# Turning q, k, similarities and one-hots on VectorE in 32 by 32 blocks instead of on TensorE

## The chip, the cores and the metric

The kernel runs on one core of one Trainium2 chip. The metric is the device time of one launch in microseconds (us). A core has five engines that run their own instruction streams side by side and wait for each other through semaphores: TensorE (PE in the profile, its weight loads PEld), VectorE (DVE), ScalarE (ACT), GpSimd (POOL) and SyncE (SP), which here only issues transfers. SBUF is the on-chip memory of 128 partitions; PSUM is the memory that TensorE writes its results to.

## The reference

Two blocks follow each other. The first is routed attention: each query and each key is assigned to the nearest of 16 centroids of its head, and a query sees only the keys of its own centroid. The second sends each of the 3072 tokens through one of 8 experts.

```python
# B, H, S, D = 4, 8, 768, 64; 16 centroids a head
q_n, k_n, c_n = (each / (its norm + 1e-6))
q_assign = np.argmax(np.einsum('bhsd,hcd->bhsc', q_n, c_n), axis=-1)
k_assign = np.argmax(np.einsum('bhsd,hcd->bhsc', k_n, c_n), axis=-1)
mask = q_assign[:, :, :, None] == k_assign[:, :, None, :]
scores = scale * np.matmul(q, k.transpose(0, 1, 3, 2))      # scale = 1/sqrt(64)
scores = np.where(mask, scores, -1000000000.0)
attn = softmax(scores)                                       # with 1e-9 in the denominator
attn_out = np.matmul(attn, v)

x = attn_out.transpose(0, 2, 1, 3).reshape(3072, 512)
expert_idx = np.argmax(x @ w_gate, axis=1)                   # 8 experts
gate_w = the softmax probability of that expert
y = np.maximum(x @ w1[expert_idx], 0.0) @ w2[expert_idx]     # 512 -> 1024 -> 512
out = gate_w[:, None] * y
```

(Shortened: norms and the softmaxes are written out in the original, and the experts work on sorted rows.)

## The kernel before

The attention stage handles two heads at a time: there are 16 pairs `g`, and each pair has 12 units (two halves of 384 queries, six blocks of 128 keys). Six units make a turn, so a pair takes two turns, an even one and an odd one. In a turn TensorE first makes six blocks of scores, then part 0 of the turn's extra jobs, then the six sums over v, then part 1 of the jobs. The two heads lie side by side in the partitions, 64 each.

The mask is made by matmul: the one-hot of a query's centroid times (one-hot of the key's centroid - 1) x 2^60 is added to the score in the same PSUM bank, so that a key of another centroid gets about -2^60 and its exponential is 0.

```python
def score(u):
    ...
    ps = ps_s.tile([P, 2, 512], F32, name="sps")                 # three buffers
    for a in range(2):                                           # L855
        nc.tensor.matmul(ps[:, a, 0:HS], lhsT=qk[g][r, 1, ks], rhs=qk[g][r, 0, qs], start=True, stop=False)
    for a in range(2):                                           # L858
        nc.tensor.matmul(ps[:, a, 0:HS], lhsT=ohT[g][r, 1, ks], rhs=ohT[g][r, 0, qs], start=False, stop=True)
    A[u] = ap.tile([P, 2, HS], F32, name="A")                    # seven buffers
    nc.scalar.activation(A[u], ps[:, :, 0:HS], AF.Exp)           # L860
    if j == 1: ... T = A[u - 1] + 1e-9 / P + A[u]                # VectorE, L863
    elif j > 1: ... T = T + A[u]                                 # VectorE, L867
```

`qk` (head dimension in the partitions, tokens along) and `ohT` (centroids in the partitions, tokens along) have to be there a turn ahead. They are made by these jobs, one after the other:

```python
def turn(g, piece):        # transposes of q and k on TensorE, eight and then four
    ...
    for i in range(n):                                           # L770
        nc.tensor.transpose(ps[:, i * P : (i + 1) * P], rows[g, "qk"[w]][:, j]..., ident)
    if piece == 0:         # L777 (VectorE; for g == 1 L775, ScalarE) q times 1/8, L778 and L780 (ScalarE) k
        ...

def similar(g):            # similarities to the centroids
    for t in range(4):                                           # L787
        nc.tensor.matmul(ps[t * 2 * C : (t + 1) * 2 * C, 0:HS], lhsT=cblk[...], rhs=qk[g][...], ...)
    nc.vector.tensor_copy(sims[g], ps[:, 0:HS])                  # L792

def similar2(g):           # three transposes (L798), and a copy on ScalarE (L800)
    ...

def assign(g):             # L806 maximum, L807 who has it, L808 (GpSimd) a rank for the first of equals
    ...
def assign2(g):            # L814 the highest rank, L818 the one-hots (twice)
    ...

def put(g):                # six transposes of one-hots on TensorE (L828)
    ...
    nc.scalar.copy(oh[:, 0, :], ps[:, 0:S])                      # L833
    for a in range(2):                                           # L835
        nc.vector.tensor_scalar(oh[a * D : a * D + C, 1, :], ..., scalar1=BIG, scalar2=-BIG, ...)
```

The sums over v, the denominators with the gate's logits, and the rows of x:

```python
def attend(u):   # L875: O += v.T @ A, two heads
def finish(g, half):   # L883, ScalarE: O to SBUF
def weigh(g):    # L896: sums of T and x @ w_gate; L902 (ScalarE): to SBUF
def weigh2(g):   # three transposes (L909), copy L912, reciprocal L918, products L921, sums L928/L931 (VectorE)
def x_turn(g, half):   # three transposes (L941), scaled by 1/denominator L944 (VectorE)
def gate(b):     # L953 to L962: the gate, once in four pairs
```

And the order of the jobs, `at(turn, part, job)`, with `n = 2 * g`:

```python
    if g == 0:   # before the first turn
        at(-4, 0, turn, g, 0); at(-4, 1, turn, g, 1); at(-3, 0, similar, g); at(-3, 1, similar2, g)
    elif g == 1:
        at(-2, 1, turn, g, 0); at(-2, 1, turn, g, 1); at(-1, 1, similar, g); at(0, 0, similar2, g)
    else:
        at(n - 3, 0, turn, g, 0); at(n - 3, 0, turn, g, 1); at(n - 3, 1, similar, g); at(n - 2, 0, similar2, g)
    at(n - 2, 0, assign, g); at(n - 2, 0, assign2, g); at(n - 1, 0, put, g)
    at(n, 1, finish, g, 0); at(n + 1, 1, finish, g, 1)
    if g < NG - 1:
        at(n + 2, 0, weigh, g); at(n + 2, 1, weigh2, g); at(n + 2, 1, x_turn, g, 0); at(n + 3, 1, x_turn, g, 1)
        ... # after each fourth pair: gate (n + 3, part 0) and the rows of x to HBM
    ...
    at(max(n - 6, -1), 1, load_qk, g); at(max(n - 5, -1), 1, load_v, g)     # from g = 2 on
```

(Several calls are put on one line here.) Towards the end of the attention stage the routing of the first three batches is worked out in the same gaps (choose, count, slots, one-hots, tokens: L582 to L656), and then the experts follow (L310 and L364 first and second layer; L476 and L498 the same as seven products in place of eight; L291 to L299 the turning of gathered rows).

Of the kernel before, what the change touches and what calls it, by code (L numbers as in the profile page):

```python
# [185 lines left out]
def kernel(  # L186
# [80 lines left out]


# [10 lines left out]
    def turn_rows(g):  # L279

        full = len([m for m in g["n"] if m == P])
        for m, j0, j1 in ((P, 0, full), (RQ, full, len(g["n"]))):
            if j0 < j1:
                nc.scalar.copy(g["gate"][0:m, j0:j1], g["xg"][0:m, j0:j1, Dm])  # L284

        for j0 in range(0, len(g["n"]), 2):
            ms = g["n"][j0 : j0 + 2]
            tp = wide().rearrange("p a (c t) -> p a c t", t=P)
            for i, m in enumerate(ms):
                for c in range(DB):  # L290
                    nc.tensor.transpose(  # L291
                        tp[:, i, c, 0:m], g["xg"][0:m, j0 + i, c * P : (c + 1) * P], ident[0:m, 0:m]
                    )
            for i, m in enumerate(ms):
                dst = g["xT"][:, :, (j0 + i) * P : (j0 + i) * P + m]
                if i == 0:
                    nc.vector.tensor_copy(dst, tp[:, i, :, 0:m])  # L297
                else:
                    nc.scalar.copy(dst, tp[:, i, :, 0:m])  # L299

    def layer1(g, fbs):
# [3 lines left out]
        for f0 in range(fbs[0], fbs[1], 2 * per):  # L305
            hp = wide()
            for fb in range(f0, f0 + 2 * per):
                o = hp[:, (fb - f0) // per, (fb - f0) % per * cols : ((fb - f0) % per + 1) * cols]
                for c in range(DB):
                    nc.tensor.matmul(  # L310
                        o, lhsT=g["w"][0][:, c, fb * P : (fb + 1) * P], rhs=g["xT"][:, c, :cols],
                        start=(c == 0), stop=(c == DB - 1),
                    )
            for a in range(2):
                dst = g["h"][:, f0 + a * per : f0 + (a + 1) * per, :cols]
                src = hp[:, a, : per * cols].rearrange("p (f t) -> p f t", f=per)
                if a == 0 and not g.get("scalar_only"):
                    nc.vector.tensor_relu(dst, src)
                else:
                    nc.scalar.activation(dst, src, AF.Relu)  # L320
# [209 lines left out]
    def place_consts():  # L530
# [23 lines left out]
        nc.gpsimd.iota(tok_i, pattern=[[S, B], [1, NQ]], base=1, channel_multiplier=NQ)  # L554
        hl_i = consts.tile([P, 2, NT], I32, name="hl_i")
# [109 lines left out]
    with ExitStack() as actx:  # L665
# [17 lines left out]
        def load_qk(g):  # L683
            b, hp = divmod(g, HP)
            for name, src in (("q", q), ("k", k)):
                t = rows[g, name] = ld.tile([P, NQ, 2, D], F32, name=name + "_in")
                for a in range(2):
                    nc.sync.dma_start(out=t[:, :, a, :], in_=src[b, 2 * hp + a].rearrange("(p j) d -> p j d", j=NQ))
# [10 lines left out]
        nc.scalar.dma_start(out=csb, in_=centroids.rearrange("h c d -> (h c) d"))  # L699
        wg_in = consts.tile([P, DB, E], F32)  # L700
        nc.scalar.dma_start(out=wg_in, in_=moe_w_gate.rearrange("(a p) e -> p a e", p=P))
        for f in (load_qk, load_v):
            for g in range(2):
                f(g)
        make_identity(nc, ident)
        nc.vector.tensor_copy(ident_b, ident)

        ps = ps_m.tile([P, 512], F32, name="mps")
        for i in range(12):
            nc.tensor.matmul(ps[:, 0:P], lhsT=ident, rhs=ident, start=True, stop=True)  # L710
# [7 lines left out]
        nc.gpsimd.memset(one_row[:, E : E + 1], 1.0)  # L718
        for a in range(2):
# [3 lines left out]
        ohs = ohp.tile([P, NQ, 2, 2, 32], BF16, name="oh")  # L723
        nc.gpsimd.memset(ohs, 0.0)
        ohTs = []
        for i in range(2):
            t = ohp.tile([P, 2, S], BF16, name=f"ohT{i}")
            nc.gpsimd.memset(t[:, 1, :], 0.0)
            ohTs.append(t)

# [3 lines left out]
        nc.scalar.activation(csq, csb, AF.Square, accum_out=cs2)  # L734
# [15 lines left out]
        cps = ps_m.tile([P, 512], F32, name="mps")  # L750
        nc.tensor.transpose(cps[:, 0:P], cn.rearrange("p a d -> p (a d)"), ident)

        cblk = consts.tile([P, HP, 2, C], F32)
        nc.gpsimd.memset(cblk, 0.0)
        cview = cps[:, 0:P].rearrange("p (g a c) -> p g a c", a=2, c=C)
        for a in range(2):
            nc.vector.tensor_copy(cblk[a * D : (a + 1) * D, :, a, :], cview[a * D : (a + 1) * D, :, a, :])
# [4 lines left out]
        def turn(g, piece):  # L762
# [3 lines left out]
            ps = ps_s.tile([P, 2, 512], F32, name="sps").rearrange("p a c -> p (a c)")  # L766
            n = 4 if piece else 8
            for i in range(n):
                w, j = divmod(8 * piece + i, NQ)
                nc.tensor.transpose(ps[:, i * P : (i + 1) * P], rows[g, "qk"[w]][:, j].rearrange("p a d -> p (a d)"), ident)  # L770
            flat = qk[g].rearrange("p w s -> p (w s)")
            if piece == 0:

                if g == 1:
                    nc.scalar.mul(flat[:, 0:S], ps[:, 0:S], D**-0.5)  # L775
                else:
                    nc.vector.tensor_scalar_mul(flat[:, 0:S], ps[:, 0:S], D**-0.5)  # L777
                nc.scalar.copy(flat[:, S:1024], ps[:, S:1024])  # L778
            else:
                nc.scalar.copy(flat[:, 1024 : 2 * S], ps[:, 0 : 2 * S - 1024])  # L780

        def similar(g):
# [8 lines left out]
            sims[g] = asg.tile([P, HS], F32, name="simT", bufs=1)  # L791
            nc.vector.tensor_copy(sims[g], ps[:, 0:HS])  # L792

        def similar2(g):
            simT = sims.pop(g)
            ps = wide()[:, 0, :]
            for i in range(NQ // 2):
                nc.tensor.transpose(ps[:, i * P : (i + 1) * P], simT[:, i * P : (i + 1) * P], ident)  # L798
            sims[g] = asg.tile([P, G, C], F32, name="sim")
            nc.scalar.copy(sims[g], ps[:, 0:HS].rearrange("p (t c) -> p t c", c=C))  # L800

        def assign(g):

            sim = sims.pop(g)
# [3 lines left out]
            nc.gpsimd.tensor_tensor(sim, sim, first_c[:, None, :].to_broadcast([P, G, C]), op=ALU.mult)  # L808
            sims[g] = sim

        def assign2(g):
            rank = sims.pop(g)
            top = asg.tile([P, G], F32, name="top")
            nc.vector.tensor_reduce(top, rank, axis=AX, op=ALU.max)  # L814

            v = lambda t, w: t.rearrange("p (i w x) c -> p i w x c", w=2, x=4)[:, :, w]
            for w in range(2):
                nc.vector.tensor_tensor(  # L818
                    ohs.rearrange("p (i h) a w c -> p i (h a) w c", h=2)[:, :, :, w, 0:C], v(rank, w),
                    top.rearrange("p (i w x) -> p i w x", w=2, x=4)[:, :, w].unsqueeze(3).to_broadcast([P, NQ // 2, 4, C]),  # L820
                    op=ALU.is_equal,
                )

        def put(g):
            oh = ohT[g] = ohTs[g % 2]
            ps = wide()[:, 0, :].bitcast(BF16)
            for j in range(NQ):
                nc.tensor.transpose(  # L828
                    ps[:, j * P : (j + 1) * P],
                    ohs[:, (j % (NQ // 2)) * 2 + j // (NQ // 2)].rearrange("p a w c -> p (a w c)"), ident_b,  # L830
                )

            nc.scalar.copy(oh[:, 0, :], ps[:, 0:S])  # L833
            for a in range(2):
                nc.vector.tensor_scalar(  # L835
                    oh[a * D : a * D + C, 1, :], ps[a * D + 32 : a * D + 32 + C, 0:S],
                    scalar1=BIG, scalar2=-BIG, op0=ALU.mult, op1=ALU.add,
                )
# [9 lines left out]
        def score(u):  # L848
# [11 lines left out]
            nc.scalar.activation(A[u], ps[:, :, 0:HS], AF.Exp)  # L860
# [43 lines left out]
        def weigh2(g):  # L904
# [7 lines left out]
            nc.vector.tensor_copy(  # L912
# [6 lines left out]
            nc.gpsimd.tensor_copy(dens[:, g, :].rearrange("p (t a) -> p t a", a=2), den)  # L919
            lgh = stat.tile([P, NQ, 2, E], F32, name="lgh")  # L920
            nc.vector.tensor_tensor(  # L921
# [5 lines left out]
            if hp == 0:  # L927
                nc.vector.tensor_tensor(lgb, lgv[:, :, :, 0, :], lgv[:, :, :, 1, :], op=ALU.add)  # L928
            else:
                for a in range(2):  # L930
                    nc.vector.tensor_tensor(lgb, lgb, lgv[:, :, :, a, :], op=ALU.add)  # L931
# [49 lines left out]
        at(0, 1, place_consts)  # L981
        for g in range(NG):
            n = g * TG
            if g == 0:
                at(-4, 0, turn, g, 0)
                at(-4, 1, turn, g, 1)
                at(-3, 0, similar, g)
                at(-3, 1, similar2, g)
            elif g == 1:

                at(-2, 1, turn, g, 0)
                at(-2, 1, turn, g, 1)
                at(-1, 1, similar, g)
                at(0, 0, similar2, g)
            else:
                at(n - 3, 0, turn, g, 0)
                at(n - 3, 0, turn, g, 1)
                at(n - 3, 1, similar, g)
                at(n - 2, 0, similar2, g)
            at(n - 2, 0, assign, g)  # L1000
            at(n - 2, 0, assign2, g)
            at(n - 1, 0, put, g)
# [317 lines left out]
```

## Time and profile before

The median of three runs is 777.45 us (776.92 to 777.67).

| engine | busy us | share of the 776.7 us span |
|---|---|---|
| TensorE, matmul | 755.2 | 97% |
| VectorE | 449.8 | 58% |
| ScalarE | 299.0 | 38% |
| GpSimd | 111.0 | 14% |

| group | count | busy us |
|---|---|---|
| L855 scores (TensorE) | 768 | 160.6 |
| L875 sums over v (TensorE) | 768 | 130.9 |
| L860 exponentials (ScalarE) | 192 | 153.3 |
| L867 sums of weights (VectorE) | 128 | 122.7 |
| L770 transposes of q and of k (TensorE) | 192 | 13.2 and 13.1 |
| L787 similarities (TensorE) | 128 | 17.8 |
| L798 transposes of similarities (TensorE) | 48 | 8.7 |
| L828 transposes of one-hots (TensorE) | 96 | 8.4 |

A row of a timeline gives the start, the time until the end of the group, the engine, the line of the kernel, the operation, and what is written and read; xN is the number of instructions. A row of the waits says who waited for whom, the total in us, how often, and the longest.

### The profile page before, as it was taken

What the parts mean: (1) busy time and instruction counts of PE and PEld (TensorE: products, weight loads), DVE (VectorE), ACT (ScalarE), POOL (GpSimd) and SP (SyncE); (2) the same over time, 40 slices, a digit from 0 to 9 for tenths busy, and PEclk for the clock granted to TensorE, in tenths of its full rate; (3) what the DMA queues carried; (4) which work ended last, traced back from release to release, by engine and by line L of the source; (5) the groups of instructions that cost most, each with busy time, mean ns of one, the idle gap of its engine ahead of it and who ended that gap; (6) DMA issues with size and microseconds to landing.
All of it is one profiled execution on the core that took longest, in us unless ns stands there. A gap on an engine that the chain in (4) does not pass through costs nothing.

```text
span 776.7 us, 12417 instructions
## 1 busy us (share of the span) xinstructions
PE 755.2 (97%) x5021; PEld 485.7 (63%) x5021; DVE 449.8 (58%) x758; ACT 299.0 (38%) x481; POOL 111.0 (14%) x157
## 2 busy tenths in 40 slices
PE   6999999999999999999999999999999999999994
PEld 4544555445554455544556668787888898787861
DVE  3667677666676666778743544555564655555200
ACT  4545645556455564555531112232222214132210
POOL 2200000100000000001200541311312121211101
PEclk9999999999999999999999999999999999999998
DMA  9025501455115221120103446747556675847540
GB/s 221 6 62 204 136 26 37 144 208 131 30 33 144 62 62 31 32 103 1 45 1 135 152 127 224 267 166 253 221 216 219 246 261 178 308 155 246 212 156 18
DMA packets 85281, 106.41 MB, mean 137 GB/s; under 512 B 52831, under 2 KB 56927, under 8 KB 84704
## 3 DMA queue, kind: packets, MB, share of 16 engines
q1 hardware_dynamic: 79616, 85.99, 34.9%
q0 software_dynamic: 4928, 19.51, 6.8%
q8 instruction: 41, 0.67, 0.4%
q14 instruction: 24, 0.20, 0.1%
q10 hardware_dynamic: 672, 0.05, 0.1%
HBM read 92.90 MB, written 13.16 MB: 137 GB/s over the span
## 4 chain that ended last, share of the span: by engine, by line
PE 80%; issue 9%; DVE 6%; POOL 2%; ACT 2%; ACTq 0%; POOLq 0%; DVEq 0%
PE sps L855 15%; PE O L875 13%; PE sps L476 10%; PE sps L310 9%; PE sps L498 8%; PE sps L364 7%; PE sps L858 4%; PE mps L896 3%; DVE T L867 3%; PE sps L787 2%; PE sps L344 2%; PE sps L770 2%; PE sps L291 2%; PE sps L941 1%; PE mps L909 1%
## 5 line engine op out<-in xcount | busy, mean ns | idle before, releaser
L860 ACT ACTIVATE A<-sps 128x768 f32<-128x768 f32 x192 | 153.3, 812 | 53.4 <-PE sps L858 52.3
L855 PE MATMUL sps<-qk 64*128 64x384 f32 x768 | 160.6, 497 | 0.1
L867 DVE TENSOR_TENSOR T<-T,A 128x768 f32<-128x768 f32 x128 | 122.7, 959 | 14.4 <-ACT lsT L902 0.5
L875 PE MATMUL O<-A,v_in 128*64 128x384 f32 x768 | 130.9, 490 | 0.0
L855 PEld LDWEIGHTS sps<-qk 64*128 64x128 f32 x768 | 66.9, 189 | 50.4 <-issue 42.3
L875 PEld LDWEIGHTS O<-A,v_in 128*64 128x64 f32 x768 | 52.2, 137 | 62.6 <-issue 62.5
L858 PE MATMUL sps<-ohT 64*128 64x384 bf16 x384 | 63.6, 325 | 0.0
L364 PE MATMUL sps<-w,h_sb 128*128 128x512 f32 x144 | 63.1, 592 | 0.0
L310 PEld LDWEIGHTS sps<-xgT,w 128*128 128x128 f32 x512 | 58.3, 192 | 4.5 <-issue 2.5
L863 DVE SCALAR_TENSOR_TENSOR T<-A 128x768 f32<-128x768 f32 x32 | 30.7, 958 | 49.1 <-ACT A L860 49.1
L310 PE MATMUL sps<-xgT,w 128*128 128x128 f32 x512 | 58.7, 275 | 0.0
L328 POOL DMA_INDIRECT out_dram<-zo,s_idx x32 | 33.3, 1041 | 154.2 <-ACT zo L324 90.9
L274 POOL DMA_INDIRECT xg<-x_rows,g_idx x32 | 37.7, 1179 | 112.8 <-ACT gate L284 100.9
L808 POOL TENSOR_TENSOR sim<-sim,first_c 128x384 f32<-128x384 f32 x16 | 16.0, 999 | 264.2 <-DVE sim L807 264.2
L364 PEld LDWEIGHTS sps<-w,h_sb 128*128 128x128 f32 x144 | 26.7, 190 | 30.6 <-issue 30.6
L883 ACT COPY xT<-O 128x384 f32<-128x384 f32 x32 | 15.5, 483 | 62.1 <-PE O L875 62.0
L476 PEld LDWEIGHTS sps<-xs,w1s 128*128 128x128 f32 x288 | 36.0, 190 | 4.2 <-DVE xs L387 4.2
L476 PE MATMUL sps<-xs,w1s 128*128 128x144 f32 x288 | 37.8, 288 | 0.0
L324 ACT ACTIVATE zo<-sps,gate 128x512 f32<-128x512 f32 x12 | 8.2, 687 | 72.1 <-PE sps L364 60.1
L858 PEld LDWEIGHTS <-ohT 64*128 64x128 bf16 x384 | 19.5, 95 | 25.3 <-issue 0.6
L297 DVE COPY xgT<-sps 128x512 f32<-128x512 f32 (+1 forms) x20 | 10.8, 566 | 40.6 <-PE sps L291 40.6
L498 PE MATMUL sps<-w2s,hs 128*128 128x256 f32 x144 | 33.6, 383 | 0.0
(246 smaller groups left out, 988.2 us busy)
## 6 DMA issues: line engine op xcount, KB each, us to landing
w<-in_moe_w_dram SPq DMA_DIRECT2D x32, 2048.0 KB, 9.2
x_rows<-x POOLq DMA_DIRECT2D x4, 1548.0 KB, 6.5
q_in<-in_q_dram SPq DMA_DIRECT2D x32, 192.0 KB, 4.4
k_in<-in_k_dram SPq DMA_DIRECT2D x32, 192.0 KB, 4.8
v_in<-in_v_dram SPq DMA_DIRECT2D x16, 384.0 KB, 3.3
xg<-x_rows,g_idx POOLq DMA_INDIRECT x32, 4.5
out_dram<-zo,s_idx POOLq DMA_INDIRECT x32, 5.5
csb<-in_centroids_dram ACTq DMA_DIRECT2D x1, 32.0 KB, 1.9
```

Of the source, the lines that this page charges most:

```text
L274: nc.gpsimd.indirect_dma_start(out=g["xg"][0:m, j, :], out_offset=None, in_=x_d[0 : g["rows"], :], in_offset=bass.IndirectOffsetOnAxis(ap= ...
L310: nc.tensor.matmul(o, lhsT=g["w"][0][:, c, fb * P : (fb + 1) * P], rhs=g["xT"][:, c, :cols], start=(c == 0), stop=(c == DB - 1),)
L328: ins = nc.gpsimd.indirect_dma_start(out=out[:, :], out_offset=bass.IndirectOffsetOnAxis(ap=g["si"](j)[0:m], axis=0), in_=zo[0:m], in_offs ...
L364: nc.tensor.matmul(zp, lhsT=g["h"][:, fb, j * P : (j + 1) * P], rhs=g["w"][1][:, fb, :], start=(fb == 0), stop=(fb == FB - 1),)
L476: nc.tensor.matmul(o, lhsT=a[:, c, f * P : (f + 1) * P], rhs=b[:, c, :], start=(c == 0), stop=(c == KH - 1),)
L498: nc.tensor.matmul(ps[:, 0, 0:DH], lhsT=a[:, f, :], rhs=b[:, f, :], start=(f == 0), stop=(f == FH - 1),)
L855: nc.tensor.matmul(ps[:, a, 0:HS], lhsT=qk[g][r, 1, ks], rhs=qk[g][r, 0, qs], start=True, stop=False)
L858: nc.tensor.matmul(ps[:, a, 0:HS], lhsT=ohT[g][r, 1, ks], rhs=ohT[g][r, 0, qs], start=False, stop=True)
L860: nc.scalar.activation(A[u], ps[:, :, 0:HS], AF.Exp)
L863: nc.vector.scalar_tensor_tensor(T[g, half], in0=A[u - 1], scalar=1e-9 / P, in1=A[u], op0=ALU.add, op1=ALU.add)
L867: nc.vector.tensor_tensor(T[g, half], T[g, half], A[u], op=ALU.add)
L875: nc.tensor.matmul(O[g, half][a * D : (a + 1) * D, 0:HS], lhsT=rows[g, "v"][:, a, j, :], rhs=a_[:, a, :], start=(j == 0), stop=(j == NQ - 1),)
```

## The change

The transposes of q, k, the similarities and the one-hots leave TensorE. VectorE has a transpose of separate 32 by 32 blocks. To make whole transposes of blocks, the rows are loaded in another order: each 32 partitions hold 32 of the 64 head dimensions of one head, in pieces of 128 bytes. The one-hots come out of VectorE in blocks that lie in other partitions than the scores want, so eight small transfers a pair carry them to `ohT`. TensorE keeps the similarity matmuls. Each step is placed behind a turn's sums of weights and a turn or more ahead of its use.

```diff
 def load_qk(g):
+    for quad in range(4 if g else 0):
+        a, d0 = quad // 2, quad % 2 * 32
+        nc.sync.dma_start(
+            out=t[quad * 32 : (quad + 1) * 32]...,
+            in_=src[b, 2 * hp + a].rearrange("(m p i) d -> p i m d", m=4, i=NQ)[:, :, :, d0 : d0 + 32],
+        )
+    for a in range(0 if g else 2):       # pair 0 as before; its k on the ScalarE queue
...
+def turn_blocks(g):
+    for w in range(2):
+        nc.vector.transpose(qk[g][:, w, :], rows[g, "qk"[w]].rearrange("p j a d -> p (j a d)"))
...
 def similar(g):
-    nc.vector.tensor_copy(sims[g], ps[:, 0:HS])
+    nc.vector.transpose(sims[g], ps[:, 0:HS])
-def similar2(g): ...
...
 def assign2(g):
-    (one-hots by two is_equal into a padded tile)
+    nc.vector.tensor_tensor(groups_of(oh), rank, top..., op=ALU.is_equal)
+    nc.vector.transpose(sims[g], oh)
+def put_q(g):
+    for half in range(2):
+        for a in range(2):
+            nc.sync.dma_start(out=ohT[g][r, 0, cols], in_=sims[g][i])
+def put_k(g):
+    for a in range(2):
+        nc.vector.tensor_scalar(kv[D:P, a, :], t[D:P], scalar1=big[...], scalar2=big[...], ...)
+    for half in range(2):
+        for a in range(2):
+            nc.sync.dma_start(out=ohT[g][r, 1, (half * HS) : (half + 1) * HS], in_=kv[i, a, :])
...
-nc.scalar.activation(A[u], ps[:, :, 0:HS], AF.Exp)
+nc.scalar.activation(A[u], ps[:, :, 0:HS], AF.Exp, scale=D**-0.5)
...
 def weigh2(g):       # the copy L912 to ScalarE, products and sums L921 to L931 to GpSimd (not in the last pair)
...
 at(...):
     if g == 0:
-        turn, similar, similar2 from turn -4 on; assign and assign2 at -2, put at -1
+        at(-4, 0, turn, g, 0); at(-4, 0, load_next); at(-4, 0, blocks); at(-4, 1, turn, g, 1)
+        at(-3, 0, similar, g); at(-3, 0, assign, g); at(-3, 0, assign2, g); at(-3, 0, put, g)
     elif g == 1:
+        at(-2, 1, idle_of, 20)           # 20 matmuls whose result is not used
+        at(0, 0, turn_blocks, g)
+        for f in (similar, assign, assign2, put_q, put_k): at(0, 1, f, g)
     else:
-        at(n - 3, 0, turn, g, 0); at(n - 3, 0, turn, g, 1); at(n - 3, 1, similar, g); at(n - 2, 0, similar2, g)
+        at(n - 3, 0, turn_blocks, g)
+        at(n - 2, 0, similar, g); at(n - 2, 0, assign, g)
+        at(n - 2, 1, assign2, g); at(n - 2, 1, put_q, g); at(n - 2, 1, put_k, g)
```

(Cut: several lines are joined, and shapes are left out. Not shown: for the first pair the transposes of q and k stay on TensorE, and its one-hots, turned in blocks too, are copied to their place by ScalarE and VectorE; the rank of the first of equals is on VectorE for pairs 0 and 1; the squares of the centroids move from ScalarE to VectorE; the loads of pair 1 and of v wait until pair 0's k has landed; some constants are placed later.) A second part concerns two evictions of one PSUM tile: where VectorE takes the first half and ScalarE the second (the turning of gathered rows, and the expert's first layer), the second is now declared independent of the first.

## The prediction

> **What bounds the kernel now.** I read the busy shares first, then who waits for whom on TensorE, then the timeline of one pair of turns, then the costs of single groups.
>
> From the page of the kernel before (part 1: engine, busy us and share; part 2: TensorE by slices):
>
> ```profile
> PE 755.2 (97%) x5021; PEld 485.7 (63%) x5021; DVE 449.8 (58%) x758; ACT 299.0 (38%) x481; POOL 111.0 (14%) x157
> PE   6999999999999999999999999999999999999994
> ```
>
> TensorE (PE) is busy in every slice but the first and the last; the others have slack. Its waits over the whole run, longest total first:
>
> ```profile
> PE sps L828 <- DVE oh L818: 2.8, 1, 2.8
> PE sps L787 <- ACT qk L778: 2.4, 4, 0.8
> PE sps L787 <- DVE qk L777: 1.6, 2, 0.9
> ```
>
> That is 6.8 us in all on these three rows, so nearly everything that the change can win is TensorE work that goes away. What that work is stands in the timeline of TensorE in the attention stage (start, us, group):
>
> ```profile
> 67.14 0.92 PE L855 MATMUL sps<-qk 64*128 64x384 f32 x4
> ...
> 72.19 0.85 PE L896 MATMUL mps<-T,one_row 128*32 128x384 f32 x8
> ...
> 73.61 0.55 PE L798 MATMUL sps<-ident,simT 128*128 128x128 f32 x3
> 74.09 4.09 PE L875 MATMUL O<-A,v_in 128*64 128x384 f32 x24
> ...
> 78.92 0.92 PE L855 MATMUL sps<-qk 64*128 64x384 f32 x4
> ...
> 83.97 0.51 PE L828 MATMUL sps<-ident_b,oh 128*128 128x128 bf16 x6
> 84.31 0.83 PE L770 MATMUL sps<-ident,q_in 128*128 128x128 f32 x6
> 84.98 0.82 PE L770 MATMUL sps<-ident,k_in 128*128 128x128 f32 x6
> 85.72 4.09 PE L875 MATMUL O<-A,v_in 128*64 128x384 f32 x24
> 89.75 0.55 PE L941 MATMUL sps<-ident,xT 128*128 128x128 f32 x3
> 90.22 0.85 PE L787 MATMUL sps<-qk,cblk 128*32 128x384 f32 x8
> 91.01 0.92 PE L855 MATMUL sps<-qk 64*128 64x384 f32 x4
> ```
>
> One head pair is two turns: an even one of 78.92 - 67.14 = 11.78 us and an odd one of 91.01 - 78.92 = 12.09 us, 23.87 us together, with no gap between groups. Starts, not durations, give the cost, since ends overlap.
>
> Some odd turns are longer. The rows at one of them (bracket: idle before, and releaser):
>
> ```profile
> 332.20 1.33 PE L787 MATMUL sps<-qk,cblk 128*32 128x384 f32 x8 [0.53 <-ACT qk L778]
> 333.46 0.92 PE L855 MATMUL sps<-qk 64*128 64x384 f32 x4
> ```
>
> [...] No row of the kernel before is such a transpose; but its ordinary VectorE passes move about one element per ns (the L867 sum of 768 takes 959 ns, the L807 pass over 384 takes 558), so I price a transpose like a pass. [...] the first scores of the kernel before start 1.76 and 1.60 us apart, later ones 0.81 (starts 18.32, 20.08, 21.68 and 30.87, 31.68 in the timeline). [...] the 32 KB of centroids took 1.9 us to land.
>
> **The change part by part, on TensorE, for a steady head pair.**
> 1. The twelve transposes of q and k go: from 84.31 to 85.72, 1.41 us.
> 2. The six of the one-hots go: from 83.97 to 84.31, 0.34 us.
> 3. The three of the similarities go: from 73.61 to 74.09, 0.48 us.
> 4. The similarity matmuls (L787, 90.22 to 91.01, 0.79 us) stay, but move from the odd turn to the even one.
>
> Even turn 11.78 - 0.48 + 0.79 = 12.09 us; odd turn 12.09 - 1.41 - 0.34 - 0.79 = 9.55 us; a pair 21.64 us, 2.23 less.
>
> From the start of turn 2 (43.27 before) the last turn included: 13 more q/k transposings x 1.41 = 18.3; 14 one-hot sets x 0.34 = 4.8; 14 similarity sets x 0.48 = 6.7; less one set of similarity matmuls that used to lie ahead of turn 2, 0.8. Sum 29.0.
>
> 5. The stalls before the similarity matmuls. At 332.20 the stretch from the end-of-turn transposes to the next score is 333.46 - 331.13 = 2.33 us, against 91.01 - 89.75 = 1.26 in an undisturbed turn: 1.07 lost. It happens at 138.6, 235.7, 332.2 and 357.9, in turns where VectorE has the gate or the routing tables and so is late with q. In the changed kernel q and k are turned a whole turn ahead; 4 x 1.07 = 4.3 us go.
>
> **On VectorE, for a pair.** Added: q and k, 2 x 0.96; the similarities out of PSUM, 0.56; the one-hots, about 0.5; the 64-partition bf16 scalings, 2 x 0.25. About 3.5 us. Removed: the scaling of q (L777) 0.96, the similarities' copy (L792) 0.56, the two mask passes (L835) 1.12, the logits' copy and arithmetic (L912, L921, L931) 0.27 + 0.26 + 0.45, and one 0.63 of one-hots becomes 0.56. About 3.7 us. So VectorE stays near its present load: 7.77 + 8.84 = 16.6 us busy in the two stretches before, over 23.87 (70%), and about the same over 21.64 (77%). By turn: even, 5.2 of sums (69.97 to 75.18) + 0.56 + 0.55 + 0.56 + 0.23 + 0.55 + 0.55 + 0.56 + 0.5 + 0.5 = 9.8 of 12.09; odd, 5.2 + 1.92 + 0.55 = 7.7 of 9.55. It fits in both.
>
> ScalarE loses L780, L778, L800 and L833 (0.59 + 0.37 + 0.48 + 0.79 = 2.2 us) and gains a copy of 0.27. GpSimd gains small sums. Neither sets anything.
>
> **The start.** Before, the first score starts at 18.32, runs at half clock, and turn 2 starts at 43.27. Afterwards q and k of pair 0 load on two queues at once, and no other load goes ahead of them; transposes at about 6.5, both evictions by 8.8, similarities by 9.7 (all estimates from rows of the same operations at 6.9 to 10.9). Then on VectorE 0.56 + 0.55 + 3 x 0.56 + 0.55 + 0.5 and four small mask pieces, one-hots about 15.0. The 20 idle matmuls fill that wait (the 12 at the start took 4.88 us cold, so 20 take 8.1 cold, about half warm) and should leave the array warm. Turn 0 is then 5.05 + 4.02 + 0.79 = 9.9, turn 1 is 9.1, and a small wait for the blocks of pair 1: turn 2 at about 34.5, that is 8.8 us earlier. This is the least sure term, +-3 us.
>
> **The expert stage.** Second halves of evictions no longer wait for the first. TensorE waited for those only 1.1 us (L310 on L299) and 0.6 us (L364 on L320) altogether; I take 0.7.
>
> Sum: 29.0 + 4.3 + 8.8 + 0.7 = 42.8; 777.45 - 42.8 = 734.6. I add 1.5 for waits that I do not see: 736.
>
> **Rivals.**
> A. VectorE becomes the bound. For it: the transposes could cost more than a plain pass, the turns are shorter, and in turns 25 to 28 the routing adds 2 to 3 us (L582 to L634). Against it: even at twice the price for the f32 transposes the odd turn has 7.7 + 1.9 = 9.6 of 9.55, and sums may lag by a turn, since seven A buffers stand behind six units. It would cost 0.1 us a pair, or with a 3 us stall in each pair some 45 us: about 778, no gain.
> B. The eight small transfers of the one-hots arrive late and take the place of the waits removed. In an even turn the chain is: sums done at 7.5, similarities 8.0, ranks with GpSimd's 1.0 by 10.3, after the output pass 12.9, then 0.55 + 0.56 + 0.5 + 0.5 to 15.0. Eight issues at about 0.37 (the rate of a v load's issue on that queue) and 2 us to land: 19.9, and the masks are needed at 21.64 + 0.6. A margin of about 2 us. If issue costs as much as a q load's 0.62, it lands at 21.9 and is still just in time; if a pair waits 1 us, that is 14 us: about 750.
> C. The loads of q and k in 128-byte pieces, twice as many packets, fall behind. Now the load of a pair keeps the transfer engines busy about 5 us (41 to 47); at double 10 us, out of 21.64. Two 2 MB weight loads stand ahead of them at turns 4 and 12, where q already took 8.19 us to issue. They have over two turns. If it fails, only those two turns pay, some 5 us each: about 745.
> D. The start gains nothing, since the chain on VectorE is long and the idle matmuls overrun it: about 743.
>
> **Range and chances.** D and part of B or C together give the upper end, 746; a better start and no hidden wait the lower, 730. Only A or B in full would bring it within 2% (above 762); I give that 5%, and slower by 2% (above 793) 1%.
>
> **What would show it.** Pairs of turns 21.6 us apart in TensorE's timeline, with no rows for q_in, k_in and the similarities' transposes in steady turns; VectorE transposes near 0.96 us (f32, 768) and 0.56 (384); TensorE's waits without L828 and with few on L858; turn 2 near 34.5. Wrong if TensorE waits for VectorE or for transfers into ohT by more than 1 us a pair, if a 768-wide block transpose takes over 2 us, or if the first scores still run at half clock.

## The result, and the profile after

The changed kernel takes 743.29 us (741.67 to 744.13) against 777.18 us (776.09 to 777.67) on the same chip: a ratio of 0.956, 95% interval 0.954 to 0.958. The prediction was 736 with a range of 730 to 746. So the direction and most of the size were right, and 7 us of the forecast were missing. The rest of the document looks for these 7 us.

The page after (part 1 and the TensorE row of part 2):

```profile
PE 719.6 (97%) x4739; PEld 461.6 (62%) x4739; DVE 453.0 (61%) x729; ACT 268.8 (36%) x435; POOL 122.9 (17%) x196
PE   8999999999999999989999999999999999999994
```

TensorE has 35.6 us less work and is still the busy engine at 97%; VectorE has 3.2 us more work, ScalarE 30 us less. But one slice in the middle, the eighteenth, is an 8 that used to be a 9. The waits of TensorE tell more:

```profile
PE sps L927 <- DVE x L1017: 6.3, 4, 3.7
PE sps L841 <- DVE cblk L799: 1.7, 1, 1.7
...
PE sps L315 <- ACT xu L304: 0.9, 1, 0.9
PE sps L371 <- ACT hs L325: 0.6, 1, 0.6
PE sps L812 <- DMA q_in<-in_q_dram: 0.3, 1, 0.3
```

From turn 2 on the waits for one-hots and for q are gone, as intended. On top stands a new one: the scores (L927 is L855 of the kernel before) wait four times for VectorE's rows of x (L1017, before L944), once for 3.7 us. Nobody reads x there. What the scores want is the PSUM bank in which the turned rows still lie.

A steady pair of turns, TensorE's timeline and of VectorE the pass over the rows of x:

```profile
57.04 0.92 PE L927 MATMUL sps<-qk 64*128 64x384 f32 x4
...
57.74 0.52 DVE L1017 TENSOR_TENSOR x<-sps,rd 128x384 f32<-128x384 f32 x1
...
58.76 0.81 PE L927 MATMUL sps<-qk 64*128 64x384 f32 x4
...
62.09 0.85 PE L968 MATMUL mps<-T,one_row 128*32 128x384 f32 x8
...
63.40 0.83 PE L841 MATMUL sps<-qk,cblk 128*32 128x384 f32 x8
64.16 4.09 PE L947 MATMUL O<-A,v_in 128*64 128x384 f32 x24
...
68.99 0.92 PE L927 MATMUL sps<-qk 64*128 64x384 f32 x4
...
74.03 4.09 PE L947 MATMUL O<-A,v_in 128*64 128x384 f32 x24
78.05 0.55 PE L1014 MATMUL sps<-ident,xT 128*128 128x128 f32 x3
78.53 0.92 PE L927 MATMUL sps<-qk 64*128 64x384 f32 x4
```

The even turn is 11.95 us, the odd one 9.54, together 21.49 in place of 23.87. The three transposing groups are gone, and there is no gap.

With three marks from the timelines (first score of turn 2, first matmul of the experts, end) the whole difference of the profiled runs falls into stages:

| stage, us | before | after | difference | predicted |
|---|---|---|---|---|
| start to turn 2 | 43.27 | 35.55 | -7.7 | -8.8 |
| turn 2 to the experts | 361.24 | 333.70 | -27.5 | -33.3 |
| experts to the end | 372.19 | 372.25 | +0.1 | -0.7 |

The missing part lies in the turns. Their lengths there are 11.95 and 9.54, except for turn 30 (13.12, as in the kernel before) and four others: 13.07 (turns 10 and 18), 13.64 (26) and 18.28 (28), which is the weak slice of the page. All engines but the weight loads at that place:

```profile
316.68 4.15 DVE L939 TENSOR_TENSOR T<-T,A 128x768 f32<-128x768 f32 x4
...
318.37 0.55 PE L1014 MATMUL sps<-ident,xT 128*128 128x128 f32 x3
...
320.74 0.97 DVE L827 STREAM_TRANSPOSE qk<-q_in 128x768 f32<-128x768 f32 x1
321.64 0.94 DVE L827 STREAM_TRANSPOSE qk<-k_in 128x768 f32<-128x768 f32 x1
...
322.57 1.35 DVE L645 TENSOR_TENSOR oh_r<-iota_f,rc 128x1152 bf16<-128x1152 f32 x1
...
323.84 0.55 DVE L1017 TENSOR_TENSOR x<-sps,rd 128x384 f32<-128x384 f32 x1
...
324.44 0.96 PE L927 MATMUL sps<-qk 64*128 64x384 f32 x4 [3.71 <-DVE x L1017]
...
325.51 1.50 PE L927 MATMUL sps<-qk 64*128 64x384 f32 x4
...
327.11 1.50 PE L927 MATMUL sps<-qk 64*128 64x384 f32 x4
...
328.66 0.81 PE L927 MATMUL sps<-qk 64*128 64x384 f32 x4
```

The lines show three things. x is turned on TensorE at 318.37, but VectorE reads it only at 323.84, because both block transposes and a routing pass stand ahead of it in VectorE's order, and because VectorE comes to them late: behind some 3 us of routing passes its sums of turn 27 end at 320.83, 11.5 us after the turn's first score, against 8.6 in the steady turn from 68.99 on. The third score of the turn starts 0.05 us after x has left its bank: three score banks go round, the rows of x take one, and the third score is the next to get it. And after the 3.7 us pause the next units of scores are 1.6 us apart (325.51, 327.11), not 0.81: from its first score to the sums (329.56) it takes 10.71 us, against 5.05 in a steady turn, 5.7 us more, with 3.7 us of waiting. In turns 10, 18 and 26 the same happens behind the gate, with 0.85 us of waiting and about 1.1 us lost (turn 26 would be 12.53 without it, as the run with another bank shows).

**Theory.** The new turns have little slack at one place: VectorE must empty the bank of x before the third score of the next turn, and the block transposes stand in front of that pass. **Rivals.** VectorE as a whole is too heavily loaded; the order alone is at fault, whichever bank; or the time is lost elsewhere (transfers, start).

### The profile page after: what moved, and what is told of

Read it like the earlier page. It is cut to its first block, busy times and chain, and to the rows that moved or that the text cites. A ratio compares the mean times of both kernels' runs of the same rounds, so it can differ in the third digit from the quotient of the medians.

```text
span 741.5 us, 12081 instructions
## 1 busy us (share of the span) xinstructions
PE 719.6 (97%) x4739; PEld 461.6 (62%) x4739; DVE 453.0 (61%) x729; ACT 268.8 (36%) x435; POOL 122.9 (17%) x196
## 4 chain that ended last, share of the span: by engine, by line
PE 81%; issue 10%; DVE 5%; POOL 1%; DMA 1%; ACT 0%; ACTq 0%; SPq 0%; POOLq 0%; DVEq 0%
PE sps L927 15%; PE O L947 15%; PE sps L483 10%; PE sps L315 9%; PE sps L505 8%; PE sps L371 7%; PE sps L930 4%; PE mps L968 3%; PE sps L351 2%; DVE T L939 2%; PE sps L841 2%; PE sps L296 2%; PE sps L1014 1%; PE mps L981 1%; POOL out_dram L335 1%
## 5 line engine op out<-in xcount | busy, mean ns | idle before, releaser
L932 ACT ACTIVATE A<-sps 128x768 f32<-128x768 f32 x192 | 152.3, 811 | 39.5 <-PE sps L930 37.9
L927 PE MATMUL sps<-qk 64*128 64x384 f32 x768 | 160.5, 496 | 6.3 <-DVE x L1017 6.3
L939 DVE TENSOR_TENSOR T<-T,A 128x768 f32<-128x768 f32 x128 | 122.7, 958 | 17.0 <-ACT A L932 3.0
L927 PEld LDWEIGHTS sps<-qk 64*128 64x128 f32 x768 | 67.1, 188 | 49.7 <-issue 33.9
L335 POOL DMA_INDIRECT out_dram<-zo,s_idx x32 | 33.3, 1041 | 155.0 <-ACT zo L331 92.2
L859 POOL TENSOR_TENSOR sim<-sim,first_c 128x384 f32<-128x384 f32 x14 | 14.0, 999 | 224.7 <-DVE sim L858 216.9
L935 DVE SCALAR_TENSOR_TENSOR T<-A 128x768 f32<-128x768 f32 x32 | 30.6, 957 | 20.1 <-ACT A L932 19.4
L990 DVE RECIPROCAL rd<-ls 128x12 f32<-128x12 f32 x16 | 3.7, 228 | 46.1 <-ACT ls L984 46.1
```

The costliest lines, as they stand in the source:

```text
L335: ins = nc.gpsimd.indirect_dma_start(out=out[:, :], out_offset=bass.IndirectOffsetOnAxis(ap=g["si"](j)[0:m], axis=0), in_=zo[0:m], in_offs ...
L932: nc.scalar.activation(A[u], ps[:, :, 0:HS], AF.Exp, scale=D**-0.5)
L935: nc.vector.scalar_tensor_tensor(T[g, half], in0=A[u - 1], scalar=1e-9 / P, in1=A[u], op0=ALU.add, op1=ALU.add)
L939: nc.vector.tensor_tensor(T[g, half], T[g, half], A[u], op=ALU.add)
```

## The experiments

All are edits of the changed kernel, and all times are medians, timed beside runs of the kernel before. Ratios are to the kernel before, with 95% intervals.

### The rows of x in another bank

```diff
 def x_turn(g, half):
-    ps = wide()[:, 0, :]
+    ps = ps_m.tile([P, 512], F32, name="mps") if half and g < NG - 1 else wide()[:, 0, :]
```

> The second half of a pair's rows of x (odd turns) is turned into the PSUM bank of the sums instead of one of the three score banks; nothing else moves, VectorE does the same passes in the same order. Theory (the third score of the next turn waits for a PSUM bank that VectorE empties late, behind the block transposes): TensorE's waits for x go from 6.3 us to nearly 0, the cold scores of turn 28 go too, 743.3 falls by about 9 (three stalls of 1.1 and one of 5.7) to 734-735. Rival 1 (VectorE itself is too late, whichever bank): the wait shows up elsewhere, at the similarities or for buffers of weights, and the time stays within 2 us of 743. Rival 2 (the lost time lies elsewhere): no change.

Measured: 734.85 us (0.946, 0.944 to 0.947), 8.4 us less than the changed kernel. TensorE's waits in this run:

```profile
PE sps L841 <- DVE cblk L799: 1.6, 1, 1.6
...
PE mps L968 <- DVE x L1017: 0.5, 1, 0.5
```

The row of 6.3 us is gone, and 0.5 us of it comes back once, in turn 28, where the sums of the same turn want the bank that x now uses. VectorE's passes and their order are the same. So the shared bank was the cause; VectorE's load and its order, which are the same here, cost this time only through it. From turn 2 to the experts it is 325.2 us, 36.0 less than before: the bank had cost 8.5 us.

### The gate and the routing behind the rows of x

```diff
-        at(n + 3, 0, gate, g // HP)
+        at(n + 3, 1, gate, g // HP)
-        at(n + 3, 0, one_hots1, 0)
+        at(n + 3, 1, one_hots1, 0)
```

> The gate (turns 9, 17, 25) and the first routing one-hots (turn 27) move behind the rows of x of the same turn; the PSUM banks stay as in the changed kernel. Theory: the three waits of 0.85 go (x comes about 1.2 us earlier than now), that of turn 27 falls from 3.7 to about 2.3 us, because VectorE is also late there from the turn before; so about 4 to 5 us less, 738 to 740. If only the order mattered, all 9 us would go (734).

Measured: 738.98 us (0.952, 0.950 to 0.953). The waits on the same bank:

```profile
PE sps L927 <- DVE x L1017: 2.3, 1, 2.3
...
PE sps L927 <- ACT A L932: 1.0, 3, 0.3
```

The three waits of 0.85 are gone and the long one is 2.3 us, as expected: VectorE still comes late out of turn 27. But three waits for ScalarE of 0.34 us are new: the gate's exponential and a copy that follows it in ScalarE's order now stand ahead of the first exponential of the turn. The order helps where the bank is tight, at a price.

### q turned twice, on either bank

```diff
 def turn_blocks(g):
-    for w in range(2):
+    for w in (0, 0, 1) if g > 1 else (0, 1):
```

> VectorE turns q of every pair from 2 on twice (0.97 us more in each odd turn, same result). Theory of the bank: in a steady turn x is out of its bank at 58.26 and the third score would want it at 58.66, so 0.4 us of slack; 0.57 us lost in nine turns and 0.97 in four, about 9 us: 752. If VectorE's load as such counted (81% busy): it has 1.5 us or more idle in each even turn, so nothing would be lost, 743.

> q twice and x in the other bank together. Theory: the 0.97 us costs nothing where no score bank hangs on it: within 1 us of the run with the other bank alone (734-735). If VectorE's capacity is the limit: 4 us or more above that run.

Measured: 758.96 us (0.977, 0.976 to 0.979) with the old bank, 736.82 us (0.948, 0.946 to 0.950) with the other. The waits with the old bank:

```profile
PE sps L927 <- DVE x L1017: 14.7, 13, 4.7
```

The same 0.97 us of VectorE work a pair, 13.6 us in 14 pairs, costs 15.7 us with the old bank and 2.0 us with the other. The slack in a steady turn was indeed less than a microsecond: the wait there is 0.41 to 0.46 us, close to the 0.57 worked out. The time was 7 us above what I expected, for two reasons. A wait of 0.46 us lengthens a turn by 0.72 (12.67 in place of 11.95), which makes some 2 us in nine turns. And two of the waits of 1.87 us were followed by units 1.6 us apart, as after the long pause: those turns (18 and 26) lost 2.7 us each over the changed kernel's, where 0.97 was expected; turn 28 lost 2.2.

With the other bank the extra work cost more than the 1 us expected, less than the 4 us that a limit of VectorE would have cost. It shows in turn 28 (14.18 against 13.17; TensorE waits 1.5 us there for x in its new bank), turn 26 (13.23 against 12.53) and twice elsewhere (0.4 and 0.2); the other turns keep their length. So VectorE's capacity counts mainly where the routing comes on top.

### q and k on TensorE again

```diff
-for quad in range(4 if g else 0):   # and the old loads for all pairs
+for quad in range(0):
-        at(n - 3, 0, turn_blocks, g)
+        at(n - 3, 0, turn, g, 0); at(n - 3, 0, turn, g, 1)
```

(With the other bank; for pair 1 likewise in turn 0.)

> From the kernel with the other bank: q and k of all pairs are loaded in the old order and turned on TensorE again (12 transposes a pair, old evictions), similarities and one-hots stay in blocks on VectorE. Theory (the gain of the steady pairs is the removed TensorE work, 1.41 us for q and k): 15 pairs x 1.41 = 21 us more than the 734.9 of the other bank, 756. Rival (transposes in a gap that TensorE has anyway, for the exponentials of the last unit): well under half of that, below 745.

Measured: 754.68 us (0.971, 0.969 to 0.972), 19.8 us more. The odd turns are 11.00 us in place of 9.54, 1.46 each. In one of them TensorE has

```profile
100.33 0.66 PE L812 MATMUL sps<-ident,q_in 128*128 128x128 f32 x4
...
101.79 4.09 PE L947 MATMUL O<-A,v_in 128*64 128x384 f32 x24
```

that is, 1.46 us from the first of the twelve transposes to the sums, without a wait. So in the odd turns the cost is TensorE's work. In the profiled runs the turns account for 18.4 us of the difference (turn 28 is 0.55 us shorter with q and k off VectorE) and the start for 2.0, turn 2 at 37.45 in place of 35.42. Beside the 42 us that the other bank's kernel gains, this part is a little under half.

### Without the idle matmuls of the start

```diff
-        at(-2, 1, idle_of, 20)
```

(With the other bank.)

> From the kernel with the other bank: without the 20 matmuls that fill TensorE's wait for the first one-hots. Theory: the first two or three units of scores run at half speed again (1.5 us each in place of 0.85), turn 2 and the end come 1.5 to 2.5 us later: 736.5 to 737.5. Rival: they overrun the wait and cost as much as they bring, 734.5 to 735.

Measured: 735.88 us (0.947, 0.945 to 0.948), 1.0 us more than the other bank alone, between the two expectations (the intervals of the two ratios overlap; the difference in turn 2 is what the traces show). TensorE's timeline at the start of this run:

```profile
10.55 0.92 PE L927 MATMUL sps<-qk 64*128 64x384 f32 x4
15.48 1.01 PE L930 MATMUL sps<-ohT 64*128 64x384 bf16 x2 [4.01 <-ACT ohT L907]
16.02 1.75 PE L927 MATMUL sps<-qk 64*128 64x384 f32 x4
...
17.78 1.42 PE L927 MATMUL sps<-qk 64*128 64x384 f32 x4
...
19.15 0.86 PE L927 MATMUL sps<-qk 64*128 64x384 f32 x4
```

After 4 us of waiting two units run slowly (1.76 and 1.37 us from start to start, where the next takes 0.80), so the effect is there. But the first unit's q-by-k part is done before the wait, which the idle matmuls prevent. Turn 2 starts at 36.03 against 35.42.

### More transfers

```diff
 def put_q(g):
+    spare = asg.tile([P, S], BF16, name="spare", bufs=1)
+    (four more transfers of the same one-hots into spare)
```

(With the other bank.)

> From the kernel with the other bank: four more transfers of the one-hots of q into a tile that nobody reads, ahead of the needed eight, 2.46 us more of issue in each pair. Slack read from the trace: the last of the eight lands at about 99.3 and the first mask of the pair is wanted at 100.6; those of the first half of the keys land at 98.4. If a unit waits for all eight: 1.1 us lost a pair, about 750. If it waits only for the half that it reads: 0.3 us, 738 to 739. If the transfers have far more room than I read (rival B of the prediction of no weight at all): 735.

Measured: 751.71 us (0.967, 0.965 to 0.968), 16.9 us more. The total is that of the first expectation, but its reason isn't. Most even turns keep their length or lose under 1 us; three lose 3.7, 6.6 and 3.4 (turns 2, 6 and 14) and the last 1.5. TensorE's largest wait, where L935 is the mask's matmul:

```profile
PE sps L935 <- DMA ohT<-kv: 9.3, 11, 2.9
```

In turns 2 and 6 units 1.6 us apart follow the wait, so these two lost more than twice what they waited (1.5 and 2.9 us). SyncE's issues for turn 6:

```profile
68.56 0.47 SPq L232 DMA_DIRECT2D w<-in_moe_w_dram  x1
69.07 0.51 SPq L237 DMA_DIRECT2D w<-in_moe_w_dram  x1
75.71 3.01 SPq L886 DMA_DIRECT2D spare<-ohs  x4
78.77 5.74 SPq L890 DMA_DIRECT2D ohT<-ohs  x4
84.60 2.44 SPq L902 DMA_DIRECT2D ohT<-kv  x4
```

Behind the weights, 4 MB in two transfers, the four issues take 5.74 us, where in a steady pair they take 2.46. So the transfers have room for most of 2.5 us more in a steady pair, and not in the two pairs that come behind weights, in pair 1 or in the last. That units wait for each half by itself fits the steady turns (0.3 us was expected, 0 to 0.9 is seen), but this run alone doesn't show it.

### Both, and an earlier start

```diff
+part_i before GpSimd's copy of the gate's weights
-for a in range(2): nc.gpsimd.tensor_copy(wg[...], wg_in[...])   # moved behind it
```

(With the other bank and the later gate.)

> The other bank and the later gate together, and the constants of the first pair ahead of GpSimd's copy of the gate's weights (which waits for its load until 7.09), so that VectorE is free for the first q at about 7.7 in place of 8.68. Theory: the similarities of pair 0 wait about 1 us less for the blocks of centroids (1.6 us now) and the whole moves by that, and the 0.5 us at turn 28 goes: 733 to 734. Rival: the start hangs on the loads of pair 1, 734.9.

Measured: 736.47 us (0.948, 0.946 to 0.949), 1.6 us slower than the other bank alone. The start did gain 0.66 us (turn 2 at 34.76), but the later gate now costs 0.62 us in each of the turns 10, 18 and 26, and turns 28 and 29 together are 0.3 us longer. ScalarE at turn 10:

```profile
122.44 0.24 ACT L1031 ACTIVATE ex<-ex 128x48 f32<-128x48 f32 x1 [5.24 <-DVE ex L1028]
122.59 0.46 ACT L955 COPY xT<-O 128x384 f32<-128x384 f32 x1
122.94 4.47 ACT L932 ACTIVATE A<-sps 128x768 f32<-128x768 f32 x6
```

Where the bank no longer waits for VectorE, putting the gate later only costs: the scores' exponentials stand behind it.

### The start alone, and evictions in order

The first run has the start of the run before and the other bank, without the later gate.

> The other bank and the earlier constants of the first pair, with the gate where the changed kernel has it. Theory: the later gate cost 0.62 us in each of four turns where the bank was already free (the gate's exponential stood ahead of the first score's on ScalarE), the start brings 0.66; so 734.1 to 734.4, 0.5 to 0.7 us below the other bank alone and about 2.3 below both_and_start. Rival: the start's gain is lost again by turn 2 (pair 1's chain), 734.9.

Measured: 734.17 us (0.944, 0.943 to 0.946), the fastest version here, 1.2% less than the changed kernel. The 0.7 us below the other bank alone lies within the intervals of the ratios, but the trace has it where it was expected: turn 2 starts at 34.57 in place of 35.42, and nothing of that is lost later.

```diff
 def apart(first, second):
-    tc.declare_no_dep(second, first, ...)
+    return
```

> The other bank, with ScalarE's half of an eviction waiting for VectorE's half as in the kernel before. Prediction's term: 0.7 us more. From the traces (the stretch from the first expert matmul to the end is 372.19 before and 372.25 after): no difference, within 0.3 us of 734.9.

Measured, with the other bank: 735.59 us (0.946, 0.945 to 0.948), against 734.85 of the other bank (the intervals of the ratios overlap). The profiled runs say where such a difference would lie: the experts take 372.2 us here and 372.3 with the independent halves, so nothing there. Turn 2 starts at 36.20 in place of 35.42, for the kernel declares the copies of the first q and k independent too: in this run's timeline ScalarE's copy of the first k (9.39) waits for VectorE's copy of the first q, which itself starts only at 8.67.

## Why the prediction was right, and where it was wrong

**Steady pairs: right.** 21.64 us were predicted and 21.49 measured. Of the three removed groups q and k were put back by themselves: 1.46 us, where the starts said 1.41. The small rest lies in the even turn, 11.95 in place of 12.09; which group it is was not tested.

**Waits before the similarities: right**, 4.3 us predicted. The kernel before has not four but five longer odd turns from turn 2 on (turn 13 by 0.2 us), together some 4.9 us, and no odd turn after is above 9.55.

**VectorE's prices: right.** The rows by shape, after:

```profile
L827 DVE STREAM_TRANSPOSE qk<-q_in 128x768 f32<-128x768 f32 x15 | 14.6, 972 | 0.0
L827 DVE STREAM_TRANSPOSE qk<-k_in 128x768 f32<-128x768 f32 x15 | 14.0, 935 | 0.0
L891 DVE TENSOR_SCALAR kv<-ohs,big 64x384 bf16<-64x384 bf16 x30 | 10.2, 386 | 0.5
L873 DVE STREAM_TRANSPOSE ohs<-oh 128x384 bf16<-128x384 bf16 x16 | 9.3, 578 | 0.6
L848 DVE STREAM_TRANSPOSE sim<-sps 128x384 f32<-128x384 f32 x16 | 9.2, 577 | 2.0 <-PE sps L841 2.0
```

960 and 560 ns were assumed. A block transpose costs nearly what an ordinary pass over as many elements costs in the same run: 972 and 935 ns for 768 in each partition, where a sum of weights (L939) takes 958, and 577 and 578 for 384, where a pass over the similarities (L858) takes 558. The 577 ns are out of PSUM and in f32, the 578 out of SBUF and in bf16. The 384 elements more cost 0.36 to 0.40 us, about 1 ns each. The mask scalings were mis-sized, 0.39 each in place of the estimated 0.25; no turn is seen to wait for that.

**Rival A: the step that failed.** The prediction compared VectorE's work in a turn with the turn's length (7.7 of 9.55) and allowed its sums to lag, "since seven A buffers stand behind six units". That is true of the sums. But VectorE also empties score banks, and there only three stand: the pass over x has to end before the third score of the next turn, some 1.7 us into it. In a steady turn that leaves some 0.5 us (x is out of its bank at 58.26, the third score starts at 58.76); behind the gate or the routing it leaves nothing. This cost 8.5 us, of which some 2 us are the slow units after the long pause. That is more than the missing 7 us: the run with the other bank, 734.9, lies at the sum worked out, 734.6, though in part because smaller errors cancel (the turns without the bank gained 36.0 us, not 33.3; the start and the experts brought 1.7 less). And that 743 us lies within the range is in part luck: its upper end, 746, was reasoned from a lost start and late transfers, D with part of B or C, and not from A.

**Rivals B and C: right in kind.** Nothing waits for one-hots in the changed kernel, but the parts of the margin were sized loosely: an issue takes 0.6 us, not 0.37, and in place of the 2 us to land (1.9 for the 32 KB of centroids in the kernel before) stand 1.8 for these 24 KB on SyncE's queue. Pairs behind weights are among the tight ones, as C supposed for the loads: with more transfers they lost 6.6 and 3.4 us (turns 6 and 14).

**The start: 1.1 us short.** Turn 2 came at 35.55 in place of 34.5. The first q waited on VectorE until 8.68, behind small constants that themselves waited for GpSimd; the run with the earlier start won 0.7 us of that. The first scores ran at full speed, as foreseen (starts at 15.31, 16.22 and 17.03, with a granted clock of 1.00), right behind the 20 idle matmuls, which took 4.73 us.

**The experts: wrong, and small.** The 0.7 us of independent evictions did not come (waits of 0.9 and 0.6 after, 1.1 and 0.6 before). What that part of the change brings is at the start: without it turn 2 comes 0.8 us later.

## What to carry to other kernels

When work moves to an engine with free time, don't ask only whether it has room in the turn. List every buffer that this engine empties for the busy one, count how many stand behind it, and see whether the new work comes ahead of that pass in its order. Here, with an engine that was busy for 61% of the span, one bank of a rotation of three let 0.97 us more work a pair cost 15.7 us in all, and a bank from elsewhere brought that down to 2.0.

## What I had not expected of the hardware

A pause of TensorE can cost more than its length: in turn 28 of the changed kernel 3.7 us of waiting cost 5.7 in all. The changed kernel around turn 28 by stretches (us, length, busy us of each engine, then the granted clock, which is the share of TensorE's full clock that it got, the share of the transfer engines and GB/s):

```profile
319.00:324.40 5.40, 1.73 (x12) 0.70 (x12) 5.29 (x8) 1.59 (x2) 1.50 (x2) 1.00 0.01 2
324.40:328.60 4.20, 4.16 (x18) 2.27 (x20) 3.63 (x5) 1.62 (x2) 2.21 (x2) 0.59 0.00 0
328.60:333.00 4.40, 4.40 (x43) 1.68 (x42) 3.64 (x6) 2.10 (x3) 0.00 (x0) 1.00 0.02 4
```

In the 4.2 us after the pause the granted clock is 0.59, and then full again. Two shorter pauses, the first in turn 2 of the run with more transfers (L932 is L927 there), the second in turn 28 of the run with the later gate:

```profile
37.61 0.32 PE L935 MATMUL sps<-ohT 64*128 64x384 bf16 x1 [1.28 <-DMA ohT<-kv]
...
38.16 1.69 PE L932 MATMUL sps<-qk 64*128 64x384 f32 x4
```

```profile
321.54 0.92 PE L927 MATMUL sps<-qk 64*128 64x384 f32 x4 [2.34 <-DVE x L1017]
...
322.45 0.81 PE L927 MATMUL sps<-qk 64*128 64x384 f32 x4
```

After 0.85 us of waiting no turn showed a slow stretch (turns 10, 18 and 26 of the changed kernel; the next units start 0.91 and 0.81 us apart). Between that and 3 us it went either way, and not by length: 1.28 us (with 0.23 more right behind them) were followed by units 1.67 and 1.60 us apart, 2.34 us by units 0.91 and 0.81 apart, and of three pauses of 1.87 us in the run with q twice turn 10 went on at full clock (1.00 from 128 to 132 us), while turn 18 fell to 0.57 (from 218 to 222) and turn 26 had units 1.36 and 1.60 us apart. Slow units followed the three longer pauses, too: 3.7 us in turn 28 above, 4.0 in the run without the idle matmuls, and 4.7 in turn 28 of the run with q twice (units 1.75 and 1.60 apart). The slow first scores of the kernel before came behind a wait, 2.77 us for the one-hots: the granted clock had been 1.00 from 5.52 to 15.76, and was 0.50 from there to 22.59, for 6.8 us. What decides for a shorter pause stays open: no run here varies that alone.
